# First piece of k through the hardware queues, free order of maxima and exponentials, and a new hand-written order

## The chip, the core and the metric

The kernel runs on one core of a Trainium2 chip. Its engines work side by side, each through its own list of instructions: TensorE (PE) for matrix products, VectorE (DVE), ScalarE (ACT), GpSimd (POOL) and SyncE (SP). They meet only at semaphores. DMAs are issued by SP and ACT (the "hardware" queues) or by POOL (the "software" queue) and are carried out by 16 DMA engines that all queues share. Products land in PSUM, which has 8 banks of 128 x 512 fp32 numbers. The metric is the device time of one execution in microseconds.

## The reference

```python
def phi(x):                                   # q, k, v: (8, 8, 576, 64); w_phi: (64, 128)
    proj = np.einsum('bhsd,df->bhsf', x, w_phi)
    proj = proj - np.max(np.abs(proj), axis=-1, keepdims=True)
    return np.concatenate([np.exp(proj), np.exp(-proj)], axis=-1)
q_p, k_p = phi(q), phi(k)
kv  = np.einsum('bhsf,bhsd->bhfd', k_p, v)
z   = np.sum(k_p, axis=2)
num = np.einsum('bhsf,bhfd->bhsd', q_p, kv)
den = np.einsum('bhsf,bhf->bhs', q_p, z)[..., None] + 1e-06
attn = num / den
x = attn.transpose(0, 2, 1, 3).reshape(4608, 512)
h = np.maximum(x @ w_in, 0.0)                 # w_in: (512, 2048)
out = h * h @ w_out                           # w_out: (2048, 512)
```

All inputs are fp32 in HBM.

## The kernel before

The eight batches (b = 0 to 7) go through a linear attention, and their 512 first tokens each make one chunk of the feed-forward part; a ninth chunk collects the 64 last tokens of every batch. Matrix products are bf16. POOL's loads turn fp32 into bf16 on the way.

For one batch, k arrives in pieces: four main pieces of two heads (`load`, L245, 128 x 512 bf16 each) and the small rest of 64 tokens (L253). Each piece becomes a group. Its 128 x 128 blocks are turned on PE (L316) against the identity `ident`, in batches 0 and 1; from batch 2 on the whole of k and q is turned by one DMA from SP (L326). The turned blocks are copied out of PSUM to `kT` (L190 on DVE or L192 on ACT), projected with `w_phi` (L369 in batch 0, L342 later), and then three instructions read the projected PSUM bank: a maximum on DVE (`mk`, L376 or L397) and two exponentials on ACT (`kp`, `kn`, L385 or L403). The maxima scale v (`em`, L416/L422, then `va`, L430), PE makes kv (L458/L463), q is treated alike (L494, L501, L572, L587, L534, L547), PE makes numerator and denominator (L651), DVE divides (L663, L677), and the result is turned to `xT` on PE or by a DMA from SP (L711). The feed-forward part multiplies by `win` (L797, and L808/L822/L836 for the first chunk), takes relu (L774 on ACT or L776 on DVE) and square (L783), multiplies by `wout` (L891), copies the result to one of three buffers `ot` (L192/L190) and stores it.

No scheduler decides the order. Every step is recorded as an `Op` in a `Plan`; the list `ORDER` says in which order the ops are issued, and so in which order each engine has them. `STATES` says which of DVE and ACT takes a copy or relu that either could do, `BASES` gives PSUM banks, `GATES` makes a load wait for a named op, and `FILL` puts products of zeros (`warm`, L964) ahead of a PE op so that PE does not rest. The numbers in these tables were found by a search outside of the kernel. Semaphores between engines follow from what is read and written; two engines that read one PSUM bank also wait for each other, in the order of the list. In POOL's list a load also waits for the landing of the load eight places ahead of it.

At the start, SP and ACT each load one half of `wphi_f` (L217), POOL loads k's pieces 2 and 3 together, then k's rest, then pieces 1 and 0, q, v and the weights.

Of the kernel before, what the change touches and what calls it, by code (L numbers as in the profile page):

```python
# [53 lines left out]
class Plan:  # L54
# [6 lines left out]
    def add(self, eng, cost, fn, r=(), w=(), opens=None, closes=None, dma=None, tiled=False, release=False, what=""):  # L61
        op = Op(eng, cost, fn, opens, closes, dma, tiled, release, len(self.ops), what)
        before = {}
# [44 lines left out]
def kernel(  # L108
# [10 lines left out]
    nc = tc.nc  # L119
# [94 lines left out]

    for half, (name, e) in enumerate((("SP", nc.sync), ("ACT", nc.scalar))):
        def fn(half=half, e=e):
            pin(e.dma_start(out=wphi_f[half * 64 : half * 64 + 64, :], in_=w_phi))  # L217
        add(name, (0.6, 2.2), fn, w=[("wphi_f", half)], what="wphi")
# [85 lines left out]
    def attention(b):  # L304
# [5 lines left out]
        def pe_transposes(x, tag, ttag, blocks, srcs, view):  # L310
# [6 lines left out]
            add("PE", pe_cost(n, 0.056), fn, r=of(tag, b, srcs) + ["ident"], opens=g, w=[g], what="T" + tag)  # L317
# [36 lines left out]
        def kgroup_ops(g):  # L354
# [7 lines left out]
            if first:  # L362
# [11 lines left out]
                def maxes(e, last):  # L374
                    def fn():
                        pin(nc.vector.tensor_reduce(  # L376
                            out=mk_view(g)[:, e, :], in_=ps1(pj[e])[:, : n * Fd].rearrange("p (i f) -> p i f", f=Fd),
                            axis=AX.X, op=ALU.max, apply_absolute_value=True))
                    add("DVE", dve_cost(n * Fd), fn, r=[pj[e]], w=[pj[e], ("mk", s2, g, e)],
                        closes=pj[e] if last else None, what="Mk")  # L380

                def exps(e, last):
                    for sgn, dst, nm in ((1.0, kp, "kp"), (-1.0, kn, "kn")):
                        def fn(dst=dst, sgn=sgn):
                            pin(nc.scalar.activation(out=dst[slot][:, e, :n, :].rearrange("p i f -> p (i f)"),  # L385
                                                     in_=ps1(pj[e])[:, : n * Fd], func=ACT.Exp, scale=sgn))
                        add("ACT", act_cost(n * Fd), fn, r=[pj[e]], w=[pj[e], (nm, slot, e)],
                            closes=pj[e] if last and sgn < 0 else None, what="E" + nm)

                maxes(0, False)  # L390
                exps(1, False)
                exps(0, True)
                maxes(1, True)
# [6 lines left out]
            add("DVE", dve_cost(2 * n * Fd), fn, r=[pj], w=[pj] + [("mk", s2, g, e) for e in range(2)], what="Mk")  # L400
            for sgn, dst, nm in ((1.0, kp, "kp"), (-1.0, kn, "kn")):
                def fn(dst=dst, sgn=sgn):
                    pin(nc.scalar.activation(out=dst[slot][:, :, :n, :].rearrange("p e i f -> p e (i f)"),  # L403
                                             in_=ps2(pj)[:, :, : n * Fd], func=ACT.Exp, scale=sgn))
                add("ACT", act_cost(2 * n * Fd), fn, r=[pj], w=[pj] + [(nm, slot, e) for e in range(2)],
                    closes=pj if sgn < 0 else None, what="E" + nm)
# [117 lines left out]
        def q_turned(c):  # L524
# [12 lines left out]
            add("DVE", dve_cost(2 * n * Fd), fn, r=[pj], w=[pj, ("mq", s2, c)], what="Mq")  # L537
            for sgn, base in ((1.0, 0), (-1.0, 2 * n * P)):
# [9 lines left out]
                add("ACT", act_cost(2 * n * Fd), fn, r=[pj], w=[pj, ("qf", f, sgn)], closes=pj if sgn < 0 else None,  # L548
# [364 lines left out]
    load(k, xk, 0, "xk", prs=((0, 1),))  # L913
# [200 lines left out]
```

## Time and profile before

| what | us |
|---|---|
| median of 3 runs | 354.33 (352.88 to 354.97) |
| the profiled execution, its own time | 353.94 |
| its span, first to last instruction | 352.2 |
| PE busy in the span | 341.5 |
| DVE busy | 268.9 |
| ACT busy | 233.3 |
| POOL busy | 96.2 |

The span is that of the engines' instructions; the 1.7 us between it and the execution's time lie around it. "Busy" of PE counts products of zeros as well, and each product until its modelled end.

### The profile page before, as it was taken

The numbers are of one execution on the slowest core, as the hardware profiler recorded it, in microseconds if no ns is written. First come the engines' busy times: TensorE is split into PE (matmuls) and PEld (weight loads), VectorE is DVE, ScalarE is ACT, GpSimd is POOL, SyncE is SP. The second block draws the span as 40 slices with busy tenths as digits, with TensorE's granted clock in tenths as the row PEclk, the third lists the DMA queues.
The fourth block names the chain that finished last, engine by engine and source line by source line (L and its number), as shares of the span: only waits on it lengthen the run. The fifth ranks groups of instructions, "written<-read, shape, count | busy, mean of one in ns | idle before, by whom it ended". The sixth has DMA issues, their size and how long they took to land.

```text
span 352.2 us, 8392 instructions
## 1 busy us (share of the span) xinstructions
PE 341.5 (97%) x3343; PEld 192.0 (55%) x3343; DVE 268.9 (76%) x513; ACT 233.3 (66%) x439; POOL 96.2 (27%) x144
## 2 busy tenths in 40 slices
PE   6999999999999999999999999999999999999995
PEld 6778866544644555445545555455555554444443
DVE  4899997889887989689979887877989653564150
ACT  3999997789885776976597785895596503212111
POOL 8673461282461636021421302040100000000000
PEclk9999999999999999999999999999999999999999
DMA  8999999999999899997999999999857431100115
GB/s 92 172 196 202 201 155 168 159 122 167 162 130 189 138 150 151 165 201 152 163 140 202 165 212 140 214 106 179 155 117 157 96 87 67 60 2 0 71 50 120
DMA packets 133623, 49.05 MB, mean 139 GB/s; under 512 B 102096, under 2 KB 129104, under 8 KB 133584
## 3 DMA queue, kind: packets, MB, share of 16 engines
q0 software_dynamic: 45232, 18.36, 46.0%
q1 hardware_dynamic: 88112, 29.99, 44.3%
q8 instruction: 26, 0.43, 0.5%
q10 hardware_dynamic: 240, 0.16, 0.2%
q14 instruction: 13, 0.11, 0.1%
HBM read 36.77 MB, written 9.44 MB: 131 GB/s over the span
## 4 chain that ended last, share of the span: by engine, by line
PE 77%; DVE 10%; ACT 5%; DMA 5%; issue 2%; SPq 0%; DVEq 0%; ACTq 0%; POOLq 0%
PE psum L797 27%; PE psum L891 27%; PE psum L651 4%; PE psum L458 4%; PE psum L342 4%; PE psum L836 2%; DMA out_dram<-ot 2%; DVE va L430 2%; DMA xT<-xo 2%; DVE mk L397 1%; ACT hr L774 1%; DMA xk<-in_k_dram 1%; DVE hr L776 1%; PE psum L572 1%; DVE h L783 1%
## 5 line engine op out<-in xcount | busy, mean ns | idle before, releaser
L891 PE MATMUL psum<-wout,h 128*128 128x512 bf16 x560 | 134.9, 379 | 0.2 <-ACT ot L192 0.2
L797 PE MATMUL psum<-xT,win 128*128 128x512 bf16 x448 | 106.9, 379 | 1.4 <-DVE hr L776 0.8
L774 ACT ACTIVATE hr<-psum 128x512 bf16<-128x512 f32 x103 | 59.8, 596 | 54.5 <-PE psum L797 36.8
L891 PEld LDWEIGHTS <-h 128*128 128x128 bf16 x560 | 50.4, 97 | 54.6 <-issue 0.9
L797 PEld LDWEIGHTS <-win 128*128 128x128 bf16 x512 | 47.6, 97 | 54.3 <-issue 2.7
L783 DVE TENSOR_TENSOR h<-hr 128x512 bf16<-128x512 bf16 x144 | 56.6, 415 | 20.6 <-ACT hr L774 19.8
L547 ACT ACTIVATE qf<-psum 128x1024 bf16<-128x1024 f32 (+1 forms) x40 | 36.5, 938 | 12.3 <-DVE mq L534 11.3
L397 DVE TENSOR_REDUCE mk<-psum 128x8 f32<-128x1024 f32 (+1 forms) x35 | 38.6, 1110 | 4.6 <-PE psum L342 4.5
L587 ACT ACTIVATE qpn<-psum 128x1024 bf16<-128x1024 f32 (+1 forms) x40 | 36.7, 938 | 5.7 <-PE psum L572 4.9
L403 ACT ACTIVATE kp<-psum 128x1024 bf16<-128x1024 f32 (+1 forms) x35 | 32.7, 935 | 9.3 <-DVE mk L397 9.2
L651 PEld LDWEIGHTS <-qpn 128*128 128x128 bf16 x624 | 27.8, 98 | 13.9 <-issue 1.0
L663 DVE TENSOR_TENSOR psum<-psum,en 128x520 f32<-128x520 f32 (+1 forms) x39 | 27.2, 701 | 9.5 <-PE psum L651 5.6
L776 DVE TENSOR_SCALAR hr<-psum 128x512 bf16<-128x512 f32 x41 | 27.8, 685 | 6.7 <-PE psum L797 6.2
L403 ACT ACTIVATE kn<-psum 128x1024 bf16<-128x1024 f32 (+1 forms) x35 | 32.8, 937 | 0.0
L651 PE MATMUL psum<-kv,qpn 128*128 128x65 bf16 x624 | 31.1, 193 | 0.0
L430 DVE TENSOR_TENSOR va<-xv,va 64x256 bf16<-64x256 bf16 (+2 forms) x66 | 30.1, 471 | 0.9 <-ACT va L422 0.2
L245 POOL DMA_DIRECT2D xv<-in_v_dram x27 | 19.7, 734 | 36.0 <-DVE h L783 11.8
L245 POOL DMA_DIRECT2D xk<-in_k_dram x28 | 20.6, 740 | 31.6 <-ACT va L422 20.0
L677 DVE TENSOR_TENSOR xo<-psum,rden 128x512 bf16<-128x512 f32 (+1 forms) x39 | 26.7, 686 | 1.4 <-DMA xT<-xo 0.7
L265 POOL DMA_DIRECT2D xq<-in_q_dram x24 | 17.4, 725 | 33.0 <-ACT hr L774 13.7
L534 DVE TENSOR_REDUCE mq<-psum 128x8 f32<-128x1024 f32 (+1 forms) x20 | 22.3, 1113 | 2.9 <-PE psum L342 2.7
L501 DVE TENSOR_REDUCE mq<-psum 128x8 f32<-128x1024 f32 (+1 forms) x20 | 22.0, 1111 | 0.9 <-PE psum L342 0.8
(79 smaller groups left out, 383.5 us busy)
## 6 DMA issues: line engine op xcount, KB each, us to landing
out_dram<-ot SPq DMA_DIRECT2D x32, 256.0 KB, 3.1
xk<-in_k_dram POOLq DMA_DIRECT2D x26, 128.0 KB, 4.6
xq<-in_q_dram POOLq DMA_DIRECT2D x24, 128.0 KB, 4.8
xv<-in_v_dram POOLq DMA_DIRECT2D x24, 128.0 KB, 4.5
win<-in_moe_w_in_dram POOLq DMA_DIRECT2D x4, 512.0 KB, 9.2
wout<-in_moe_w_out_dram POOLq DMA_DIRECT2D x4, 512.0 KB, 14.0
xq<-in_q_dram POOLq DMA_DIRECT2D x4, 256.0 KB, 7.1
out_dram<-ot SPq DMA_DIRECT2D x6, 128.0 KB, 2.4
```

Of the source, the lines that this page charges most:

```text
L245: pin(nc.gpsimd.dma_start(out=x[:, a * 512 : z * 512].rearrange("p (h x) -> p h x", x=4 * D), in_=src[b][2 * a : 2 * z, 0:512, :].rearrang ...
L397: pin(nc.vector.tensor_reduce(out=mk_view(g), in_=ps2(pj)[:, :, : n * Fd].rearrange("p e (i f) -> p e i f", f=Fd), axis=AX.X, op=ALU.max, ...
L403: pin(nc.scalar.activation(out=dst[slot][:, :, :n, :].rearrange("p e i f -> p e (i f)"), in_=ps2(pj)[:, :, : n * Fd], func=ACT.Exp, scale= ...
L430: pin(nc.vector.tensor_tensor(out=t[:, :, :D].rearrange("p m (x c) -> p m x c", c=2), in0=x.rearrange("p (m x c) -> p m x c", m=n, c=2), i ...
L547: pin(nc.scalar.activation(out=o, in_=i_, func=ACT.Exp, scale=sgn))
L587: pin(nc.scalar.activation(out=o, in_=i_, func=ACT.Exp, scale=sgn))
L651: pin(nc.tensor.matmul(out=o[:, u // 4, u % 4 * D1 : (u % 4 + 1) * D1], lhsT=qpn[slot][:, sg * half + u * m : sg * half + u * m + P], rhs= ...
L774: pin(nc.scalar.activation(out=hr[sl], in_=ps1(g), func=ACT.Relu))
L776: pin(nc.vector.tensor_scalar(out=hr[sl], in0=ps1(g), scalar1=0.0, scalar2=None, op0=ALU.max))
L783: pin(nc.vector.tensor_tensor(out=dst, in0=i_, in1=i_, op=ALU.mult))
L797: pin(nc.tensor.matmul(out=o, lhsT=win[mc // 4][:, kc, mc % 4 * P : (mc % 4 + 1) * P], rhs=x, start=(kc == 0), stop=(kc == KC - 1)))
L891: pin(nc.tensor.matmul(out=ps1(g), lhsT=h2[c % 2][mc // 4][:, mc % 4, tt * P : (tt + 1) * P], rhs=wout[mc // 4][:, mc % 4, :], start=(mc = ...
```

## The change

The first main piece of k of batch 0 is no longer loaded by POOL. Its two halves are loaded in fp32 by SP and by ACT, ahead of `w_phi`, into the output buffer `ot[2]`, which is free at that time; one half is then cast to bf16 into `xk` by ACT and one by DVE (`kcast`). Its group is the first that PE turns. The maximum and the exponentials of a group no longer have a fixed order in the plan: they only share a lock on the bank. `ORDER`, `BASES`, `STATES`, `GATES` and `FILL` are new throughout. POOL's first instructions become: k pieces 2 and 3, `ident`, k piece 1, the first half of q, k's rest, the second half of q, v. Products of zeros go from 123 to 143; 26 of them still stand ahead of the first turn.

```diff
+    for hi, (name, e) in enumerate((("SP", nc.sync), ("ACT", nc.scalar))):
+        def fn(hi=hi, e=e):
+            pin(e.dma_start(out=ot[2][:, 256 * hi : 256 * hi + 256],
+                            in_=k[0][hi, 0:512, :].rearrange("(p j) d -> p (j d)", j=4)))
+        add(name, (0.58, 2.35), fn, w=[("xkf", hi)], what="xkh")
...
-            add("PE", pe_cost(n, 0.056), fn, r=of(tag, b, srcs) + ["ident"], opens=g, w=[g], what="T" + tag)
+            halves = [("xkh", hi) for hi in range(2)] if first and tag == "xk" and srcs == [0] else of(tag, b, srcs)
+            add("PE", pe_cost(n, 0.056), fn, r=halves + ["ident"], opens=g, w=[g], what="T" + tag)
...
-                    add("DVE", dve_cost(n * Fd), fn, r=[pj[e]], w=[pj[e], ("mk", s2, g, e)],
-                        closes=pj[e] if last else None, what="Mk")
+                    add("DVE", dve_cost(n * Fd), fn, r=[pj[e]], w=[("mk", s2, g, e)], lock=pj[e], what="Mk")
...
-                add("ACT", act_cost(2 * n * Fd), fn, r=[pj], w=[pj] + [(nm, slot, e) for e in range(2)],
-                    closes=pj if sgn < 0 else None, what="E" + nm)
+                add("ACT", act_cost(2 * n * Fd), fn, r=[pj], w=[(nm, slot, e) for e in range(2)], lock=pj, what="E" + nm)
...
-    load(k, xk, 0, "xk", prs=((0, 1),))
+    for hi in range(2):
+        def f_kcast(hi=hi):
+            copy(xk[0][:, 256 * hi : 256 * hi + 256], ot[2][:, 256 * hi : 256 * hi + 256])
+        o = add("DVE", dve_cost(256), f_kcast, r=[("xkf", hi)], w=[("xkh", hi)], what="kcast")
+        plan.either((o, "ACT", act_cost(256)))
+    load(k, xk, 0, "xk", prs=())
...
 ORDER = [
...
```

Of the 40 groups of k, the maximum stands ahead of both exponentials in 39 before and in 18 after; it stands between them in 12 and behind both in 10 after. Relu on DVE goes from 41 to 48 chunks, the copy to `ot` on DVE from 15 to 10.

More of the change, by code (lines that the diff above doesn't have):

```diff
@@ L59, in __init__, with add @@
         self.groups, self.banks = 0, []
-    def add(self, eng, cost, fn, r=(), w=(), opens=None, closes=None, dma=None, tiled=False, release=False, what=""):
+    def add(self, eng, cost, fn, r=(), w=(), opens=None, closes=None, dma=None, tiled=False, release=False, what="", lock=None):
         op = Op(eng, cost, fn, opens, closes, dma, tiled, release, len(self.ops), what)
+        op.lock = lock
         before = {}
@@ L372, in kgroup_ops, with maxes @@
                     opens=tuple(pj), tiled=True, what="Pk")
-                def maxes(e, last):
+                def maxes(e):
                     def fn():
@@ L378, in fn, with exps @@
                             axis=AX.X, op=ALU.max, apply_absolute_value=True))
-                    add("DVE", dve_cost(n * Fd), fn, r=[pj[e]], w=[pj[e], ("mk", s2, g, e)],
-                        closes=pj[e] if last else None, what="Mk")
-                def exps(e, last):
+                    add("DVE", dve_cost(n * Fd), fn, r=[pj[e]], w=[("mk", s2, g, e)], lock=pj[e], what="Mk")
+                def exps(e):
                     for sgn, dst, nm in ((1.0, kp, "kp"), (-1.0, kn, "kn")):
@@ L386, in fn @@
                                                      in_=ps1(pj[e])[:, : n * Fd], func=ACT.Exp, scale=sgn))
[L387 to L393, printed above, removed]
+                        add("ACT", act_cost(n * Fd), fn, r=[pj[e]], w=[(nm, slot, e)], lock=pj[e], what="E" + nm)
+                maxes(0)
+                exps(1)
+                exps(0)
+                maxes(1)
                 return
@@ L399, in fn @@
                     axis=AX.X, op=ALU.max, apply_absolute_value=True))
-            add("DVE", dve_cost(2 * n * Fd), fn, r=[pj], w=[pj] + [("mk", s2, g, e) for e in range(2)], what="Mk")
+            add("DVE", dve_cost(2 * n * Fd), fn, r=[pj], w=[("mk", s2, g, e) for e in range(2)], lock=pj, what="Mk")
             for sgn, dst, nm in ((1.0, kp, "kp"), (-1.0, kn, "kn")):
@@ L536, in fn @@
                     axis=AX.X, op=ALU.max, apply_absolute_value=True))
-            add("DVE", dve_cost(2 * n * Fd), fn, r=[pj], w=[pj, ("mq", s2, c)], what="Mq")
+            add("DVE", dve_cost(2 * n * Fd), fn, r=[pj], w=[("mq", s2, c)], lock=pj, what="Mq")
             for sgn, base in ((1.0, 0), (-1.0, 2 * n * P)):
@@ L547, in fn @@
                     pin(nc.scalar.activation(out=o, in_=i_, func=ACT.Exp, scale=sgn))
-                add("ACT", act_cost(2 * n * Fd), fn, r=[pj], w=[pj, ("qf", f, sgn)], closes=pj if sgn < 0 else None,
+                add("ACT", act_cost(2 * n * Fd), fn, r=[pj], w=[("qf", f, sgn)], lock=pj,
                     what="Eqp" if sgn > 0 else "Eqn")
@@ L970 @@
 ORDER = [
[84 rows of a table removed]
[84 rows of a table added]
 ]
 BASES = (
-    '6416400204322513661766422322303066244004212225500116560364052321520063666262060671046174450554510220'
-    '0074766200632320030044545745044406625177535353421636126466346124271707562172030220124656661401142406'
-    '0521060023272401407337722555000322023644665716064116141117701024024564166263266207446420070114711526'
-    '2200223265026500450054435750413426075473330556731234357527705727215016742316316745263'
+    '1460050163241512534622510033002441064366046005522116446520422511326664222662444470326375541445112642'
+    '6107714364441440222620030106367135260566420206423020564406560600177221767374452463344000647763236300'
+    '2066222335677526625544546002543361200662624542304246443104502314406117126006664451771135120240200033'
+    '1364420210624632535673436027722171070404003434202055450011373530002153571042674606357'
 )
 STATES = (
-    '0000000101000111101000110010000000000000010000011100110000100010001000101001010001000010110010100010'
-    '0000100100100101010000000000100100100001100100101000011101000000000100101011101000000100010110001000'
-    '1101100110001011100000011011000'
+    '1000000110000000111000000101100010000000010001000011010001000000010110000000000000101000001100110100'
+    '0010100001100000000000010011100100100000011110011000001100000101001011010100000000110100011111100100'
+    '111001011101010010010001000111000'
 )
 GATES = {
[11 rows of a table removed]
[11 rows of a table added]
 }
 FILL = {
-    85: (0, 26), 87: (0, 4), 63: (7, 27), 65: (7, 10), 112: (7, 4), 108: (7, 3), 110: (7, 3), 116: (7, 23),
-    147: (0, 5), 144: (3, 5), 228: (5, 2), 139: (7, 7), 135: (7, 4),
+    44: (0, 26), 46: (0, 9), 77: (0, 20), 79: (0, 6), 113: (7, 3), 53: (7, 15), 55: (7, 13), 68: (7, 4), 109: (7, 6),
+    111: (7, 3), 119: (7, 23), 147: (7, 4), 133: (3, 3), 142: (7, 6), 239: (0, 2),
 }
```

190 rows, old and new, of tables (GATES, ORDER) are left out of this document.

## The prediction

> **What bounds the kernel now.** I read the page's shares and slices first, to see where PE is not at work.
>
> ```profile
> PE 341.5 (97%) x3343; PEld 192.0 (55%) x3343; DVE 268.9 (76%) x513; ACT 233.3 (66%) x439; POOL 96.2 (27%) x144
> PE   6999999999999999999999999999999999999995
> DVE  4899997889887989689979887877989653564150
> ACT  3999997789885776976597785895596503212111
> ```
>
> PE idles 352.2 - 341.5 = 10.7 us, and the group L964 (products of zeros) holds another 11.4 us of its "busy" time, all of it ahead of 27 us. So the room is at the start. The windows show who fills it.
>
> ```profile
> 0.00:5.00 5.00, 2.87 (x26) 2.69 (x26) 1.25 (x6) 1.28 (x1) 3.91 (x10) 1.00 0.49 64
> 5.00:10.00 5.00, 4.28 (x57) 3.87 (x58) 3.78 (x9) 2.80 (x7) 5.00 (x8) 0.71 1.35 130
> 10.00:15.00 5.00, 4.88 (x79) 4.18 (x78) 3.89 (x11) 4.51 (x13) 3.74 (x6) 0.95 1.55 171
> 15.00:20.00 5.00, 4.15 (x48) 2.56 (x46) 4.96 (x10) 4.96 (x13) 1.70 (x3) 1.00 1.50 194
> 20.00:25.00 5.00, 5.00 (x110) 4.19 (x109) 5.00 (x10) 5.00 (x13) 4.89 (x7) 1.00 1.50 192
> ```
>
> The columns are PE, PEld, DVE, ACT and POOL busy, the granted clock, DMA share, GB/s. From 15 to 25 us DVE is busy 9.96 of 10 us and ACT 9.96: these two, not PE, set the pace until PE is dense at about 30 us. What either does earlier there should carry to the end. From 30 to 300 us PE is busy 266.83 of 270. The timeline tells when the two begin.
>
> ```profile
> 0.74 0.57 SPq L217 DMA_DIRECT2D wphi_f<-in_w_phi_dram  x1
> 0.99 2.87 PE L964 MATMUL psum<-warm 128*128 128x128 bf16 x26 [0.99 <-DVE warm L226]
> 1.24 0.87 POOL L245 DMA_DIRECT2D xk<-in_k_dram  x1 [0.80 <-POOLq L1098]
> 1.35 1.28 ACT L385 ACT_TABLE_LOAD   x1 [1.35 <-PEq L1098]
> 5.72 0.86 PE L316 MATMUL psum<-ident,xk 128*128 128x128 bf16 x10 [1.85 <-DMA xk<-in_k_dram]
> 6.15 0.95 DVE L190 COPY kT<-psum 128x512 bf16<-128x512 bf16 x3 [2.11 <-PE psum L316]
> 7.20 1.45 ACT L385 ACTIVATE kp<-psum 128x512 bf16<-128x512 f32 x3 [4.57 <-PE psum L369]
> 8.07 2.82 PE L964 MATMUL psum<-warm 128*128 128x128 bf16 x27
> 11.16 0.42 DVE L190 COPY kT<-psum 128x512 bf16<-128x512 bf16 x1 [1.01 <-PE psum L316]
> ```
>
> POOL's first load, issued at 1.24, lands 4.4 us later; PE, DVE and ACT wait for it. The last line is a second stall of DVE, behind 27 products of zeros. Landings of the hardware queues, for the piece that moves, are in the issues list:
>
> ```profile
> out_dram<-ot SPq DMA_DIRECT2D x32, 256.0 KB, 3.1
> out_dram<-ot SPq DMA_DIRECT2D x6, 128.0 KB, 2.4
> xk<-in_k_dram POOLq DMA_DIRECT2D x1, 256.0 KB, 4.4
> wphi_f<-in_w_phi_dram SPq DMA_DIRECT2D x1, 32.0 KB, 2.2
> wphi_f<-in_w_phi_dram ACTq DMA_DIRECT2D x1, 32.0 KB, 2.4
> ```
>
> **The early piece.** Each half is 128 KB in fp32, issued at 0.74. Bounds for its landing are the 32 KB row (2.2, so 2.9) and the 256 KB row (3.1, so 3.9, both halves flying at once); I take 3.3, near the 128 KB row. The DVE cast lies between the cast of `wphi_f` (128 x 128, 0.24) and a copy of 128 x 512 (0.42): 0.35. ACT issues two DMAs now (0.58 each), so its table load of 1.28 ends at 1.93 + 1.28 = 3.2; its cast costs about the 0.45 of a 128 x 256 exponential, to 3.75. The 26 zero products end at 3.87, so the four turns (0.39) start then, not at 5.72. DVE copies at about 4.3, where it was 6.15: 1.8 us sooner. ACT's first exponential, 1.48 behind the first turn before, comes at 4.9 to 5.3, not at 7.20: 2.1 us sooner. Both casts lie in time in which their engines waited (1.96 us on DVE, 4.57 on ACT): nothing. Without that cover they would cost 0.35 and 0.45.
>
> Not all of this lead is kept. The first group feeds DVE 0.42 + 2 x 0.64 = 1.7 us, until 6.1, and ACT four exponentials of about 0.5, until 7.2. The next groups need POOL's load, issued at 1.24 as before, so landing at 5.7 or a little later beside the new traffic, and PE has 9 + 20 zero products in the way, so their copies come at 6.6. By then DVE had done 0.45 us of copies before and 1.7 now: lead 1.25; ACT's lead is 2.0. I take **1.3** (bounds 0.7, by one load below, and 2.0).
>
> **Moved issues.** `wphi_f` goes out 0.57 later on both queues and lands by 3.7, its cast ends by 4.1, and the first projection needs it at 4.8: nothing; if it were late, all of the lead would go with it. `ident` is made at about 2.1 on POOL, ahead of k's piece 1 (0.35 us), and must be: the turn needs it at 3.9, and before it was ready at 5.18. POOL issues one load fewer (0.76), so later loads may land about 0.7 us sooner, but a DMA share of 1.35 or more from 5 us on says that bytes bind too. The first product with `win` starts at 28.6, 5.9 behind the first landing (issued at 13.5, 9.2 under way): zero (0 to 0.7). k's rest moves behind half of q, 3 us later or so; it is needed only for kv at 21 us: zero.
>
> **The second stall.** DVE's 1.01 at 11.16 is PE's 27 zero products at 104 ns each (2.82 / 27), while 23 later ones took 1.45 us. Now the largest block behind the first group has 23, at the same place as before, ahead of the q projections, but k's rest comes later and can stall DVE in its turn. I take half, **0.5** (0 to 1.0).
>
> The slow block ran under a granted clock of 0.71 in that window, following PE's idle 1.85 us. The Trainium skill, "TensorE: Matmul & The Clock Gate", Part 1, says that the clock is halved after a window with too little work. The trace agrees in the order of these events; by that rule no gap means no slow block, and this term would be the full 1.0 and the sum 0.5 lower.
>
> **Twenty more zero products** cost 20 x 0.06 = 1.2 us only if PE is late there; PE waits for DVE and ACT: zero (loss up to 1.2).
>
> **The rest of the order.** DVE takes 7 more relus (0.685) and 5 fewer copies of `ot` (about 0.6): +1.8 us on a 268.9 that has 83 us of room: zero. What PE waits for after 30 us and a free order of readers can reach is the wait for `kn` L403, 0.3. I take **0.3** from bounds of 3.2 won (all of PE's idle from 30 to 300) and 3.2 lost.
>
> Sum: 1.3 + 0.5 + 0.3 = 2.1 us. From the profiled 353.94 that gives **351.8**, which is 0.7% under the median of 354.33. About 0.5%, or 1.8 us, is what a measurement here can tell from no change.
>
> **Rival: the lead is absorbed.** If the landings, not DVE and ACT, set the pace, the early piece gains only what the stream of loads loses, one load of about 0.7 us: 353.2, no difference that can be told. For it: DMA share of 1.35 to 1.55 from 5 to 25 us. Against: the two engines at 99.6% in the same time. The Trainium skill, "DMA: Bandwidth & Descriptors", section "Issuing engines are not separate DMA queues", says that issuing from several engines saves only sequencer time; that would be this case. The rows for a 128 KB store and a 256 KB load, 2.4 and 4.4, neither confirm nor refute it, as sizes differ. It also covers an ACT half that comes late. Chance 0.27.
>
> **Rival on the other side: maxima behind the exponentials.** In 10 of the 40 groups of k the maximum now comes last, so it waits for two exponentials of 0.94: 1.9 us later into the chain `mk` (1.11), `em`, `va` (0.69), kv. Where PE reaches kv with less than 1.9 us to spare, it stalls for the difference. At two such groups in dense batches with nothing to spare, 3.8 us would be lost and the lead with it halved (1.0): 353.94 + 3.8 - 1.0 = 356.7; from one and a half such stalls on the change is a loss. For it: `mk` and `va` both stand in the chain that ended last (1% and 2%). Against: PE waited for neither after 30 us, and the exponentials then need less waiting (ACT L403 idled 9.2 us for `mk`). Chance 0.18.
>
> **A better case:** ACT's full lead of 2.0, the whole stall and half of the 3.2: 349.3. Chance 0.10. The forecast keeps 0.45.
>
> **Numbers.** Faster takes the forecast and the better case less a share of the forecast that ends within 0.5%: 0.53. Same is the rival of absorption and that share: 0.29. Slower is the last rival: 0.18. The range reaches from under the better case, 348.8, to the rival of slower, 356.6.
>
> **What would show it.** First turn at 3.9 and first `kT` copy at 4.3; first exponential near 5; DVE without the idle microsecond near 11; the dense stretch some 2 us sooner, and PE idle from 30 to 300 near 3 us. Wrong: a first turn after 4.5, DVE idle over 1 us between 6 and 12, or PE idle past 30 us grown by over 2.

## The result, and the profile after

| | before | after |
|---|---|---|
| median of 20 executions each, us | 354.46 (352.64 to 359.51) | 352.38 (350.22 to 358.01) |
| ratio of the times | 1 | 0.9944, interval 0.9925 to 0.9963 |
| the profiled execution, us | 353.94 | 352.64 |
| its span, us | 352.2 | 350.9 |

The change makes the kernel 0.56% faster, 2.0 us by the ratio. The longest executions (one of before, three of after) were in a slower state, which the ratio leaves out. The forecast was 351.8, from a sum of 2.1 us. The total is right; two of the three terms that it was summed from are not, and most of what follows is about that.

The page's shares and slices of the kernel after:

```profile
PE 338.6 (97%) x3331; PEld 192.0 (55%) x3363; DVE 270.4 (77%) x519; ACT 232.2 (66%) x435; POOL 95.4 (27%) x143
PE   7999999999989999999999998999999999999995
DVE  3999999899868978798879995889789836652530
ACT  3999997798968898876877866886477402111321
```

PE is busy for 2.9 us less than before although there are 20 more products of zeros (part of it is 32 product records that are missing here: 3331 beside 3363 weight loads), and the second and seventh slices of DVE went from 8 and 7 tenths to 9. The windows of the kernel after, with the same columns as before:

```profile
0.00:5.00 5.00, 3.96 (x36) 3.59 (x37) 0.96 (x4) 1.70 (x2) 3.86 (x10) 1.00 0.57 89
5.00:10.00 5.00, 4.01 (x73) 3.45 (x72) 3.22 (x8) 2.92 (x6) 4.47 (x7) 1.00 1.67 171
10.00:15.00 5.00, 4.85 (x80) 4.06 (x78) 5.00 (x12) 4.95 (x16) 4.50 (x7) 1.00 1.52 191
15.00:20.00 5.00, 4.38 (x81) 3.63 (x79) 4.93 (x11) 4.99 (x13) 3.01 (x5) 1.00 1.55 192
20.00:25.00 5.00, 4.83 (x96) 3.92 (x93) 4.97 (x10) 4.66 (x12) 3.54 (x6) 1.00 1.43 195
```

DVE and ACT are saturated from 10 us on, where before it was from 15. But from 5 to 10 us, where the early piece should have shown, DVE has done less than before (3.22 against 3.78). The timeline of the kernel after says why.

```profile
0.74 0.40 SPq L218 DMA_DIRECT2D ot<-in_k_dram  x1
1.19 0.56 SPq L224 DMA_DIRECT2D wphi_f<-in_w_phi_dram  x1
3.52 0.42 ACT L193 ACTIVATE xk<-ot 128x256 bf16<-128x256 f32 x1 [0.47 <-DMA ot<-in_k_dram]
3.69 0.50 DVE L191 CAST xk<-ot 128x256 bf16<-128x256 f32 x1 [2.68 <-DMA ot<-in_k_dram]
3.99 0.64 PE L323 MATMUL psum<-ident,xk 128*128 128x128 bf16 x4
5.64 0.62 DVE L228 CAST wphi<-wphi_f 128x128 bf16<-128x128 f32 x1 [1.18 <-DMA wphi_f<-in_w_phi_dram]
6.07 0.36 DVE L191 COPY kT<-psum 128x512 bf16<-128x512 bf16 x1
6.92 0.60 ACT L392 ACTIVATE kn<-psum 128x512 bf16<-128x512 f32 x1 [2.98 <-PE psum L377]
9.61 1.29 DVE L384 TENSOR_REDUCE mk<-psum 128x4 f32<-128x512 f32 x2 [0.49 <-PE psum L377]
```

The first turn starts at 3.99, 1.73 us sooner than before. Then `w_phi` is late: issued second on each queue, it lets DVE wait until 5.64, the first `kT` copy comes at 6.07 (before: 6.15) and the first exponential at 6.92 (before: 7.20). Almost all of the lead is gone in one instruction. What `w_phi` took is in the answer for its line, over both halves (shortest, median, longest), with the row of POOL's first load from the issues list:

```profile
DMA to landing us min/median/max: 2.7/3.5/4.4
xk<-in_k_dram POOLq DMA_DIRECT2D x1, 256.0 KB, 5.4
ot<-in_k_dram SPq DMA_DIRECT2D x1, 128.0 KB, 2.8
```

Before, the halves of `w_phi` took 2.2 and 2.4, and POOL's 256 KB 4.4.

To see where a lead is kept, I lined the traces up by work done. Each non-zero product was weighted by its columns (0.216 us for 512, pairs of 64-row products counted once, 311.6 us in all), and the table gives the start of the weight load at which the same amount had been done, as a difference to the profiled execution of before. It is worked out from the records of the weight loads, which are complete in every trace (products are not). The rows compare unlike mixes of products: the row at 25 us moves by up to 0.5 us, alike in all columns but e8, when the products of 64 rows are weighted in another way. So only differences of a microsecond, steps between neighbouring rows, and differences between columns of the same list mean much.

| work done (clock of before) | after | the same again, e0 | e2 | e6 | e8 |
|---|---|---|---|---|---|
| 4 us (20.1) | -1.79 | -2.64 | -2.27 | -2.41 | -0.89 |
| 25 us (45.7) | +0.08 | -0.75 | -0.72 | -0.86 | -0.89 |
| 80 us (106.8) | -1.05 | +0.50 | -1.43 | -3.32 | -0.87 |
| 160 us (192.8) | -2.77 | -0.76 | -3.14 | -4.82 | -1.77 |
| 308 us (344.8) | -1.40 | -0.92 | -1.70 | -5.23 | -1.77 |

In the profiled execution of after the start is worth next to nothing by 45 us (at most 0.4, by other weights), and what it wins comes later. e0 is the same kernel in another execution; the other columns are explained below.

### The profile page after: what moved, and what is told of

Read it like the earlier page. It is cut to its first block, busy times and chain, and to the rows that moved or that the text cites. A ratio compares the mean times of both kernels' runs of the same rounds, so it can differ in the third digit from the quotient of the medians.

```text
span 350.9 us, 8415 instructions
## 1 busy us (share of the span) xinstructions
PE 338.6 (97%) x3331; PEld 192.0 (55%) x3363; DVE 270.4 (77%) x519; ACT 232.2 (66%) x435; POOL 95.4 (27%) x143
## 4 chain that ended last, share of the span: by engine, by line
PE 81%; DVE 7%; DMA 7%; ACT 2%; issue 1%; SPq 0%; DVEq 0%; ACTq 0%
PE psum L896 30%; PE psum L802 30%; PE psum L656 5%; PE psum L350 4%; DMA qpn<-qf 4%; PE psum L463 4%; PE psum L841 2%; DMA qT<-xq 2%; DVE va L435 2%; DMA wphi_f<-in_w_phi_dram 1%; DVE mq L506 1%; DVE mk L384 1%; PE psum L813 1%; PE psum L577 1%; PE psum L860 1%
## 5 line engine op out<-in xcount | busy, mean ns | idle before, releaser
L896 PE MATMUL psum<-wout,h 128*128 128x512 bf16 x528 | 129.8, 379 | 2.2 <-ACT kp L409 0.5
L779 ACT ACTIVATE hr<-psum 128x512 bf16<-128x512 f32 x96 | 55.8, 597 | 46.8 <-PE psum L802 33.5
L896 PEld LDWEIGHTS <-h 128*128 128x128 bf16 x560 | 51.3, 97 | 56.1 <-issue 0.8
L781 DVE TENSOR_SCALAR hr<-psum 128x512 bf16<-128x512 f32 x48 | 32.4, 682 | 12.5 <-PE psum L802 12.0
L193 ACT ACTIVATE ot<-psum 128x512 f32<-128x512 f32 x25 | 14.7, 598 | 30.3 <-PE psum L896 28.0
L656 PEld LDWEIGHTS <-qpn 128*128 128x128 bf16 x624 | 27.2, 97 | 13.0 <-issue 1.2
L656 PE MATMUL psum<-kv,qpn 128*128 128x65 bf16 x624 | 30.4, 193 | 0.1
L539 DVE TENSOR_REDUCE mq<-psum 128x8 f32<-128x1024 f32 (+1 forms) x20 | 22.1, 1110 | 3.8 <-PE psum L350 3.1
```

Source lines behind the costliest of these rows:

```text
L656: pin(nc.tensor.matmul(out=o[:, u // 4, u % 4 * D1 : (u % 4 + 1) * D1], lhsT=qpn[slot][:, sg * half + u * m : sg * half + u * m + P], rhs= ...
L779: pin(nc.scalar.activation(out=hr[sl], in_=ps1(g), func=ACT.Relu))
L781: pin(nc.vector.tensor_scalar(out=hr[sl], in0=ps1(g), scalar1=0.0, scalar2=None, op0=ALU.max))
L896: pin(nc.tensor.matmul(out=ps1(g), lhsT=h2[c % 2][mc // 4][:, mc % 4, tt * P : (tt + 1) * P], rhs=wout[mc // 4][:, mc % 4, :], start=(mc = ...
```

## The experiments

Three groups ran, each beside runs of before (27, 22 and 18 executions, medians 353.39, 353.14 and 353.56). Ratios are to before.

**Again, and `w_phi` first.** The kernel after was run again (e0), and once with `w_phi` issued ahead of k's halves (e1):

```diff
 ORDER = [
-    0, 1, 17, 2, 3, 11, ...
+    2, 3, 17, 0, 1, 11, ...
```

> The changed kernel again, as the yardstick for the three kernels beside it on the same chip. Every theory: 0.994 of the kernel before, 352.4 us; the later half of w_phi lands after 5 us again and the first copy to kT starts near 6.1 us.

> Only the two issues on SP and on ACT change places: w_phi goes out ahead of the halves of k. Theory A (the early piece's lead was lost because a half of w_phi landed at 5.5 us, and would carry to the end if kept): w_phi lands by 3.2, k's halves by 4.2, first copy to kT by 5.2 instead of 6.07, first exponential by 6.0 instead of 6.92, and the end 0.5 to 1.0 us sooner than the changed kernel. Rival B (the start is set by the next groups' landing near 6.6 us and by the stream of loads, so the first group's time is worth nothing): first copy and exponential as sooner as that, but the end within 0.3 us of the changed kernel.

e0: 0.9963 (0.9934 to 0.9993). e1: 0.9985 (0.9962 to 1.0007). In the traced execution of e0, `w_phi` landed sooner (its cast at 4.46, first `kT` copy at 4.88, first exponential at 5.96), and the end still lay only 0.92 ahead. e1 gains nothing over e0; its timeline:

```profile
1.36 0.87 ACTq L218 DMA_DIRECT2D ot<-in_k_dram  x1
3.77 0.42 ACT L193 ACTIVATE xk<-ot 128x256 bf16<-128x256 f32 x1 [0.23 <-DMA ot<-in_k_dram]
5.34 0.29 DVE L191 CAST xk<-ot 128x256 bf16<-128x256 f32 x1 [4.33 <-DMA ot<-in_k_dram]
5.69 0.39 PE L323 MATMUL psum<-ident,xk 128*128 128x128 bf16 x2 [1.05 <-DVE xk L191]
6.19 0.36 DVE L191 COPY kT<-psum 128x512 bf16<-128x512 bf16 x1
```

Now `w_phi` is there in time (2.85 and 3.50), and one half of k, second on ACT's queue, takes 3.96 us; the other, second on SP's, 2.38. The `kT` copy is as late as with `w_phi` behind. So what stands second on a queue can be late whatever it is, but only on one of the two, and not always: in after it was SP's half of `w_phi` (4.36 beside 2.66), in e9 ACT's (4.29 beside 2.79), in e0 neither (3.03 and 3.25). Whether the place or POOL's load beside it makes one late, no run separates.

**The order alone.** e2 keeps the whole new order and takes the early piece out: POOL loads the piece in bf16 as its first load, 128 KB, and both casts are left out.

```diff
-            pin(e.dma_start(out=ot[2][:, 256 * hi : 256 * hi + 256], ...
+            if hi == 0:
+                pin(nc.gpsimd.dma_start(out=xk[0][:, 0:512]..., in_=k[0][0:2, 0:512, :]...
...
-            copy(xk[0][...], ot[2][...])
```

> The new order is kept, the early piece undone: POOL loads k's first piece in bf16 as its first load, and both casts are left out. Theory A (most of the 2 us comes from the new order past 40 us, not from the early piece): slower than the changed kernel by at most 0.7 us, still 1.3 us or more under the kernel before; w_phi lands near 3 us again. Rival C (the early piece pays through the stream of loads, one load shorter): all landings behind it 0.7 us later, and at least 1.5 us slower than the changed kernel, so level with the kernel before.

0.9940 (0.9921 to 0.9960): no slower than the full change. Its timeline:

```profile
1.25 0.82 POOL L219 DMA_DIRECT2D xk<-in_k_dram  x1 [0.80 <-POOLq L1110]
3.13 0.23 DVE L230 CAST wphi<-wphi_f 128x128 bf16<-128x128 f32 x1 [1.84 <-DMA wphi_f<-in_w_phi_dram]
4.45 0.61 PE L325 MATMUL psum<-ident,xk 128*128 128x128 bf16 x4 [0.50 <-DMA xk<-in_k_dram]
5.09 0.42 DVE L191 COPY kT<-psum 128x512 bf16<-128x512 bf16 x1 [1.45 <-PE psum L325]
```

POOL's first load lands after 3.15 us when it has 128 KB, not after the 4.4 of its 256 KB. The hardware queues are worth 0.46 us at the first turn (4.45 against 3.99) and nothing that can be told at the end. The column e2 above: 0.72 ahead at 45 us, as e0 with 0.75.

Where that 0.46 goes can be seen, since e0 and e2 have the same list. PE's second turn is at 6.99 in e0 and 7.45 in e2, and e0 is still 0.37 us ahead on PE, DVE and ACT at 26 us. Then comes one instruction of DVE, first in e0, then in e2:

```profile
26.77 0.71 DVE L668 TENSOR_TENSOR psum<-psum,en 128x520 f32<-128x520 f32 x1 [0.38 <-ACT qpn L592]
26.73 0.71 DVE L670 TENSOR_TENSOR psum<-psum,en 128x520 f32<-128x520 f32 x1
```

In e0 it waits for the end of an exponential that began at 25.66; in e2 the same exponential begins at 26.03, and DVE does not wait for its end. From 30 to 60 us the two traces are level to 0.05 us. After, e1 and e9, which have the early piece, wait there as well (0.36 us each); e5, e6, e7, e10 and e12, which do not, never. So the gain of the hardware queues ends in one wait, and not in a late landing. Why only the kernel with the early piece has it, and whether the end would keep the 0.4 us without it, no run shows.

**Maxima first.** e4 keeps the change but moves each maximum of a turned group in `ORDER` to just ahead of its first exponential, in the 22 of 40 groups of k and the 8 of 20 of q that did not have it there (in outline; `Ekp` and `Mk` stand for op numbers).

```diff
 ORDER = [
-    ..., Ekp g, ..., Mk g, ...
+    ..., Mk g, Ekp g, ...
```

> In every group of k and of the turned q the maximum is put ahead of both exponentials again, all else of the new order kept. Theory A (the rest of the new order pays, and the free order of maxima is part of it): 0.5 to 1.5 us slower than the changed kernel, with ACT waiting more for mk and mq. Rival D (the free order is worth nothing by itself, or costs by pushing the scaling of v later): within 0.3 us of the changed kernel, or faster.

1.0719 (1.0694 to 1.0744), 25 us slower. What ACT waited for from 30 to 300 us in e4:

```profile
ACT kn L409 <- DVE mk L403: 16.5, 8, 3.3
ACT kp L409 <- DVE mk L403: 14.8, 12, 2.5
ACT qf L552 <- DVE mq L539: 11.2, 8, 3.6
```

and in before, in its own numbering:

```profile
ACT qf L547 <- DVE mq L534: 11.3, 9, 2.5
ACT kp L403 <- DVE mk L397: 9.2, 11, 2.4
```

In e0 ACT waits 1.5 us in all for maxima of k past 30 us, and 1.3 for those of q. So putting the maxima last is no price that this order pays: exponentials that go first spare it waits. The 25 us is not the worth of the free order, though, since the rest of the list was not arranged anew around the moved maxima.

**Two stalls of the new order.** The waits of PE in the kernel after name what it lost on the way:

```profile
PE psum L577 <- DMA qT<-xq: 1.3, 1, 1.3
PE psum L350 <- ACT qf L552: 1.1, 1, 1.1
PE psum L377 <- DVE kT L191: 1.0, 1, 1.0
```

The third is the late `w_phi`. The first is at 103 us: SP's list has the turning of q by DMA behind another one, which waited 9.8 us for DVE, and a store.

```profile
94.66 1.19 SPq L716 DMA_TRANSPOSE xT<-xo  x1
95.94 0.53 SPq L914 DMA_DIRECT2D out_dram<-ot  x1
96.70 3.52 SPq L334 DMA_TRANSPOSE qT<-xq  x1
```

The second is at 214 us, behind ACT's wait for a buffer that a DMA still reads (`qpn<-qf`). e6 takes e2 and moves that turning of q (op 596) ahead of the other one (op 468):

```diff
 ORDER = [
-    ..., 468, ..., 596, ...
+    ..., 596, 468, ...
```

e5 takes e2 and lets the fifth chunk of a turned q use a buffer of its own; e7 has both edits.

```diff
+            buf = qf[f] if c < 4 else otl[:, :].bitcast(BF16)
...
-                    o = qf[f][:, base : base + 2 * n * P]
+                    o = buf[:, base : base + 2 * n * P]
```

> New order with POOL's first piece (as e2_pool_first), and in the turned batches 4 to 7 the last chunk of q gets a buffer of its own (the idle tail output buffer), so that the exponentials into qf wait less often for the DMA that reads it. Theory A (the lead that the new order has at 180 us of useful PE work, 4.2 us in e2, is lost to ACT's wait for that DMA near 212 us): the wait of ACT at qf falls from some 4 us to under 1.5, the lead at 200 us of useful work stays above 2.5 us, and the end is 1 us sooner than e2, near 350.2. Rival B (the DMA-turned q of that stage is late whoever holds the buffer, because SP issues its turns one after another): the wait moves to qpn, end within 0.4 us of e2.

> As e2_pool_first, but SP's turn of q of batch 3 (issued at 95.9, landed at 103.5, PE stalled 1.7 to 2.3 us for it in three profiles of the new order) stands ahead of the one xT turn and the one store that were ahead of it. Theory A: issued near 93, landed by 100.5, the stall is gone; of its 1.7 us at most 0.5 reaches the end, because the stage near 212 us takes leads away. Rival B (nothing takes leads away): the end is 1.5 us sooner than e2. Rival C: the xT turn, 3.6 us later, becomes the stall: no gain or slower.

> Both edits together. Theory A: where each alone gives at most 1 us, both give 2 us or more against e2, 349.3 or below, 0.988 of the kernel before. Rival: no better than the better one of the two.

e6: 0.9885 (0.9855 to 0.9915), its interval wholly below that of e2. e7: 0.9890 (0.9854 to 0.9926). e5: 0.9945 (0.9916 to 0.9973), inconclusive: three of its executions ended near 349.6 and the rest from 351.6 on. In e6 SP goes like this:

```profile
90.49 4.39 SPq L336 DMA_TRANSPOSE qT<-xq  x1
94.97 1.22 SPq L718 DMA_TRANSPOSE xT<-xo  x1
```

PE's wait for `qT` is gone from its list, and ACT's waits for `qpn<-qf` are 0.25 near 207 us, where after had 1.67 at 212, and 0.75 near 225, where e2 had 2.60 at 228. In this trace the second stall has gone with the first, which would explain why e7 adds nothing to e6. But it does not always go: in the trace of e9 (below), which has the same move, ACT waits 2.26 us for `qpn<-qf` at 208.6 and PE 1.96 at 211.

**Products of zeros.** e8 is before with 17 zero products fewer in the block that follows the first group.

```diff
-    85: (0, 26), 87: (0, 4), 63: (7, 27), 65: (7, 10), ...
+    85: (0, 26), 87: (0, 4), 63: (7, 10), 65: (7, 10), ...
```

> The kernel before with 10 instead of 27 products of zeros ahead of the turn of k's piece 1, nothing else. The prediction's second-stall term: DVE's idle 1.01 us near 11 us goes, and 0.5 to 1.0 us of it reaches the end, so 0.997 to 0.9985 of the kernel before. Rival (leads of the start are absorbed before 50 us, as the new order's lead of 1.5 us at 20 us was gone at 47 us): DVE and the first q projections come 0.5 to 1 us sooner, the end is unchanged within 0.3 us, or later if the clock is granted at half longer.

0.9976 (0.9959 to 0.9993), 0.85 us. The column e8 above is the clearest of all: 0.89 ahead from the first row on, unchanged for 87 us of run (its further 0.9 by the fourth row are two waits of before's profiled execution at 108.5 and 109.9 us, for `ot` and `qpn`, that e8 does not show). So in a list that stays the same, a lead of the start does carry to the end. The 0.89 itself is not the price of the 17 products alone, as the two traces differ in the clock too: in before it went back to half from 7.06 to 10.48 us, in e8 it did not. The price is the 0.85 of the times.

**The move once more, with and without the early piece.** e12 is e6 again; e9 makes the same move in the kernel after; e10 is e6 with other counts of zero products, 31 in place of 26 ahead of the first turn and 8 in place of 20 behind the first group:

```diff
-    44: (0, 26), 46: (0, 9), 77: (0, 20), ...
+    44: (0, 31), 46: (0, 9), 77: (0, 8), ...
```

e11, beside them, is before with 43 in place of 26 ahead of the first turn:

```diff
-    85: (0, 26), 87: (0, 4), 63: (7, 27), ...
+    85: (0, 43), 87: (0, 4), 63: (7, 27), ...
```

> e6_xq_sooner once more, as the yardstick for the kernels beside it: 0.9885 of the kernel before, 349.1 us.

> The changed kernel with its early piece, and SP's turn of q of batch 3 moved as in e6. Theory A (the early piece is worth nothing, the moved turn is worth about 2 us whatever the start): within 0.7 us of e12_xq_again, so 0.987 to 0.991 of the kernel before. Rival (the early piece pays once the later stall is gone): at least 1 us sooner than e12_xq_again.

> e6 with 31 instead of 26 products of zeros ahead of the first turn (PE idled 0.5 us there) and 8 instead of 20 ahead of the turns of k's pieces 2 and 3. Theory A (in some executions PE's full clock comes only at 9 to 10 us, and zero products counted for the full clock then hold the turns back by 1 to 2 us): the median 0.3 to 1.0 us under e12_xq_again and a narrower spread. Rival: the turns wait for landing and DVE anyway, within 0.3 us.

> The kernel before with 43 instead of 26 products of zeros ahead of its first turn, so that PE does not idle the 1.85 us until k lands. Theory A (that idle time is what brought the half clock from 7.1 to 10.5 us, and with it slow zero products and DVE's second stall): no half clock after the first full clock, DVE's second stall under 0.3 us, 0.5 to 1.0 us under the kernel before. Rival (the half clock depends on where its window happens to lie, and most executions of the kernel before have none): within 0.3 us.

e12: 0.9902 (0.9863 to 0.9941). e9: 0.9923 (0.9892 to 0.9954). e10: 0.9891 (0.9869 to 0.9913), with executions from 349.48 to 350.74. e11: 0.9993 (0.9975 to 1.0010). The early piece buys nothing here either: e9 is 0.002 above e12, as e0 was 0.002 above e2; both pairs of intervals overlap. e6, e10 and e12 are faster than both kernels by their ratios, about 3.5 to 4 us under before; the interval of e12, alone of the three, overlaps those of after and e2.

e11 fills PE's idle 1.85 us ahead of the first turn, to see whether the block behind it then runs at full clock. Its windows:

```profile
5.00:10.00 5.00, 4.14 (x75) 3.49 (x73) 3.63 (x9) 2.64 (x7) 5.00 (x8) 1.00 1.31 131
10.00:15.00 5.00, 3.02 (x49) 2.20 (x47) 3.02 (x8) 4.30 (x12) 3.68 (x6) 0.96 1.58 178
15.00:20.00 5.00, 4.92 (x49) 3.99 (x49) 4.72 (x10) 3.55 (x10) 2.27 (x4) 0.70 1.49 193
```

It does: 1.00 where before had 0.71, and DVE, behind the same 27 products of zeros, does not idle between 6.3 and 12.3 us, where before had its 1.01. But PE then idled 0.93 and 1.13 us up to 12.7 and 15.1, and the clock was 0.70 in the next window. This trace is of the slowest of e11's 12 executions; by their ratio the time did not change.

## Why the prediction was right in total and wrong in two terms

That the sum came out is luck. The 1.3 us that the early piece did not bring are made up by about 1.0 more from the order and 0.35 more from the second stall than they were sized at.

**The early piece: sized 1.3, measured nothing.** Landings of the halves were taken as 3.3 and came at 3.50 and 3.67; the casts took 0.50 on DVE and 0.42 on ACT where 0.35 and 0.45 were taken; the first turn was put at 3.87 and came at 3.99. The step that failed is the next: "lands by 3.7 ... nothing; if it were late, all of the lead would go with it". It landed at 3.83 on one queue and 5.54 on the other, and the lead went. I had priced it by the row of a queue that carried nothing else. But this is not the whole: in e0, with `w_phi` there 1.2 us sooner, 0.75 us is left at 45 us, and e2 without the early piece has 0.72. The second fault is thus in what it was compared with. The words "the four turns (0.39) start then, not at 5.72" set the new path against a 256 KB load; the new order also makes POOL's first load smaller, and a 128 KB load is there 1.3 us sooner by itself. What two more queues add to that is 0.46 us at the first turn, and DVE's wait near 27 us takes it back. A third reading was off as well: POOL's load of pieces 2 and 3, put at 5.7 "or a little later", landed at 6.63 (6.77 in e0), so the next copies, put at 6.6, came at 8.37 (7.41 in e0).

**The second stall: sized 0.5, measured 0.5 to 0.9.** e8 prices the block of zero products alone at 0.85 us (0.25 to 1.45 by its interval). After, DVE's idle 1.01 has become 0.49. This is the likeliest content of the 0.75 that e0 and e2 hold at 45 us; no run shows that directly. The profiled execution of after holds next to nothing of it. The term was read from an execution that is not the usual one: a stretch of 3.4 us at half clock takes 1.7 of 352 us from the mean granted clock, so to 0.995, as in the profiled execution of before, and 54 of the 67 executions of before beside the experiments had 0.998 or more. In the trace of e11, which has no such stretch there, DVE's 1.01 us is gone. How the 17 products cost 0.85 us in an execution without it, no trace shows.

The sentence on the clock, that no gap means no slow block, was half right (its "sum 0.5 lower" should read the time; the sum would be 0.5 higher). e11 has no gap there and no slow block there, but in its trace a slow stretch came 8 us later, and the time stayed. The Trainium skill, "TensorE: Matmul & The Clock Gate", Part 1, calls the window of the clock free-running; the runs agree, in that one and the same start met it differently from execution to execution (below).

**The rest of the order: sized 0.3 (between 3.2 lost and 3.2 won), measured 0.2 to 1.8, about 1.** Past 45 us the lists with the new order and q's turning at its place gained 1.48 (after), 0.17 (e0), 1.83 (e1) and 0.98 (e2) on the profiled execution of before, 1.1 in the mean; up to 0.9 of it is that execution's own loss near 110 us, so that by the traces alone 0.2 to 1.1 are left. The times say 1.3: e2, the order without the early piece, wins 2.1 us, less the 0.85 of e8, if the new order has all of that. I had looked only at PE's waits for something worth winning. Those did not shrink: summed from 30 us on they are 3.1 us in before and 3.8 in after. One thing that did shrink stands in no list of waits. PE's timeline after shows it:

```profile
104.84 1.89 PE L896 MATMUL psum<-wout,h 128*128 128x512 bf16 x8
106.56 0.41 PE L656 MATMUL psum<-kv,qpn 128*128 128x65 bf16 x8
106.81 1.03 PE L896 MATMUL psum<-wout,h 128*128 128x512 bf16 x4
107.77 0.39 PE L577 MATMUL psum<-qT,wphi 64*128 64x512 bf16 x2
108.00 0.40 PE L350 MATMUL psum<-wphi,qT 64*128 64x128 bf16 x8
108.33 0.42 PE L656 MATMUL psum<-kv,qpn 128*128 128x65 bf16 x8
```

Read the starts, not the busy times. Eight products of `wout` ahead of L656, which takes all 128 rows as they do, need 106.56 - 104.84 = 1.72, 0.215 each. Four ahead of L577, whose products take 64 rows, need 107.77 - 106.81 = 0.96, which is 0.10 more than 4 x 0.215. The eight 64-row products of L350 come in pairs of 0.056; the way out of them, 108.33 - 108.00 = 0.33, is 0.11 more than 4 x 0.056. Over all 35 such places of before past 30 us, the step into 64 rows took 0.311 at the median where 512 columns otherwise took 0.216. One trip into 64-row products and out again so costs 0.2 us, and the page counts it as busy. From 30 us on the old order makes 51 such trips and the new one 46 (62 and 58 over the whole run): 5 x 0.2 = 1.0 us. Counts and spacing are read from the traces; no run changed the number of trips alone, so that this is the order's gain is worked out and not shown. The Trainium skill, "TensorEngine Tiling (Array Packing)", section "Tiling Modes", says that a change of the tiling mode drains TensorE; the spacing agrees, with 0.2 us for both changes.

**The rivals.** "The lead is absorbed" described the outcome of the early piece rightly, though not by the stream of loads as a whole: a transfer second on its queue did it in after, and DVE's wait near 27 us in e0. The Trainium skill, "DMA: Bandwidth & Descriptors", section "Issuing engines are not separate DMA queues", says that issuing from several engines saves only sequencer time; that fits a gain of 0.46 us at the first turn and none at the end (e2, e9). The rival missed the order. "Maxima behind the exponentials" is refuted: the change was no loss, and e4, with the maxima first, lost 25 us. Of the three signs named as wrong, the first turn (3.99) and DVE's idle (0.52 at the longest) held. The third, PE idle from 30 to 300 us grown by over 2, was met on paper: 3.17 became 5.23. It was a bad sign to name: 28 product records are missing in that stretch, and the hole that one leaves can count as idle; by the list of waits the growth is 0.7.

**Still open**: what the free order, the new landings and the new search each give of the order's microsecond; whether e5's buffer helps; and whether e10's zero products do, since its median lies within the spread of e6 and e12.

## What to carry to other kernels

Price a transfer by its place on its queue and by what flies beside it, and compare a new path with the same size on the old one, before giving a queue the credit. An order may gain where no engine waits: look at the spacing of products at each change of their kind, not only at the list of waits. Two traces of one list show where a lead ends: compare them instruction by instruction. After a large rearrangement read PE's few longest waits: one transfer that stood behind another that waited was worth 1.3 to 1.9 us (e2 to e12 and e6), nearly as much as the whole change.

## What the runs showed of the hardware that was not expected

- Second on a hardware queue, beside POOL's first load, 32 KB took 2.7 to 4.4 us (after, e0, e9) where it took 2.0 to 2.8 first on the queue (before, e1, e2), and 128 KB took 2.38 and 3.96 (e1) where the halves of after, first on theirs, took 2.76 and 2.93.
- POOL's first load took 3.15 us with 128 KB (e2) and with 256 KB 4.4 (before) to 5.6 (e9).
- Going from 128-row to 64-row products and back costs PE 0.2 us (0.10 and 0.11), without a gap in the busy time.
- The traces' records of the clock first have it full at 3.65 us in before, 5.26 in after, 8.97 in e1 and 5.18 and 10.1 in two executions whose first 8 us have the same instructions (e6, e7). In e7 twenty zero products took 2.31 us in place of 1.29, and the next turn came at 8.68 in place of 7.31. The windows' column of the clock reads 1.00 before that too (0 to 5 us above), though the first 26 zero products of before took 2.87 us there, 0.11 each, and 23 later ones 1.45, 0.06 each.
- In e9 the clock went back to half at 212 us, behind PE's wait of 1.96 us (granted clock 0.72 from 210 to 215 us).
